# Two small changes at the ends of a fused attention and MLP kernel: the later packed queries load by a casting DMA on the GpSimd queue, and the last output tile is made as two column halves stored from two queues

## The chip, the cores and the metric

The kernel runs on one core of a Trainium2 chip. The metric is the device time of one execution in microseconds; lower is better. "The span" is the part of an execution that the profile covers, about 2 us shorter. "Same" means within 2%, so both the prediction and the result are about differences of about one per cent, and the traces carry the argument.

Engine names as the profile has them: PE is the tensor engine's matmuls, PEld its weight loads, DVE the vector engine, ACT the scalar engine, POOL the GpSimd engine, SP the engine that here only issues DMAs. POOLq, SPq and ACTq are the sequencers of those engines while they issue DMAs.

## The reference

For each of 8 batches and 8 heads, 32 packed queries `p` attend over 576 keys and values. The result serves as keys and values for the 576 queries `q`. Then a two-layer MLP with squared ReLU follows.

```python
def sm_attn(qq, kk, vv):                       # softmax attention, scale 1/8
    ...
p_packed = sm_attn(p, k, v)                    # p: 8 x 8 x 32 x 64
out = sm_attn(q, p_packed, p_packed)           # q, k, v: 8 x 8 x 576 x 64, float32
x = out.transpose(0, 2, 1, 3).reshape(4608, 512)
h = np.maximum(x @ w_in, 0.0)                  # w_in: 512 x 2048
return (h * h) @ w_out                         # w_out: 2048 x 512, output 4608 x 512 float32
```

## The kernel before

The program is written as streams of steps (load, transpose, scores, MLP matmuls and so on). When it is built, a small list scheduler (`Plan`) places the steps by assumed durations, and the order of their planned starts becomes the order of the instructions on each engine. Engines then run in order and wait on semaphores. So a step's assumed duration or its place in a stream can change the order of everything after it.

q, k, v, w_in and w_out are cast to bf16 by DMAs on the GpSimd queue, at most eight in flight, since each such load waits for the completion of the one eight before it. The packed queries are loaded in two parts, batches 0 and 1 first and batches 2 to 7 ("later p") afterwards. p is then transposed on DVE (`tr_p`) and expanded into a block-diagonal tile `pT_bd` on POOL (`expand_p`). The first score matmuls of a batch (`ps_a<-pT_bd,kT`) read that tile. Output tile t is 128 tokens x 512 columns, made of 16 matmuls (`f2_mm`).

```python
p_f = {}
def load_p(b0, b1, eng):                                     # float32, rows of 64 elements
    n = (b1 - b0) * NQD
    p_f[b0] = stg.tile([P, 2 * B, D], F32, name="p_f", tag="p")[:, :n, :]
    eng.dma_start(p_f[b0], p[b0:b1].rearrange("b (qd h) i d -> (h i) (b qd) d", h=QH))
def cast_p(b0, b1, eng):                                     # to bf16, on DVE
    ...
def tr_p(b0, b1):
    nc.vector.transpose(pT[:, b0 * NQD:b1 * NQD], p_b[b0].bitcast(F32))
def expand_p(b, eng):                                        # POOL for b > 0
    for h in range(QH):
        cast(eng, bd2(pT_bd[b % 2], h), pT[32 * h:32 * h + 32, ...]...)
# ... [cut]
def f2_out(t, eng):                                          # eng: ACT or DVE
    ob[t] = opool.tile([P, NE], F32, name="o_sb")
    cast(eng, ob[t], po[t])
    for i in range(4):
        b, j = divmod(t * 4 + i, JT)
        dst = out[b * S:(b + 1) * S, :].rearrange("(a j) e -> j a e", j=JT)[j]
        nc.sync.dma_start(dst, ob[t][32 * i:32 * i + 32, :])
# ... [cut]
def pload(b0, b1):
    if b0 == 0: ...                                          # ACT queue
    return Step(f"LP.{b0}", [stage([("SP", 0.45, lambda: load_p(b0, b1, nc.sync))]),
                             stage([("DMA", 1.6, lambda: None)])], [], [("p", 1)], (), lag=1.6)
ld = load_steps(0) + w_in_load() + w_out_load()[:2] + load_steps(1) + w_out_load()[2:]
for b in range(2, B):
    ld += load_steps(b) + ([pload(2, B)] if b == 2 else [])
```

The softmax here doesn't subtract the row's maximum and nothing guards it: scores larger than these inputs give would overflow.

Of the kernel before, what the change touches and what calls it, by code (L numbers as in the profile page):

```python
# [9 lines left out]
ACT = mybir.ActivationFunctionType  # L10
ALU = mybir.AluOpType
F32 = mybir.dt.float32
BF16 = mybir.dt.bfloat16

P = 128
D = 64
NP = 32
QH = 4
JT = 18
# [268 lines left out]
def kernel_impl(tc, q, k, v, p, w_in, w_out, out):  # L288
    nc = tc.nc
    B, H, S, Dh = q.shape  # L290
# [3 lines left out]
    NE = w_out.shape[1]  # L294
    NFB = DFF // FB
# [5 lines left out]
    NKQ = 8  # L301
    NT = TOK // P

    with ExitStack() as ctx:
        ctx.enter_context(tc.manual_schedule())
        consts = ctx.enter_context(tc.tile_pool(name="consts", bufs=1))
        stg = ctx.enter_context(tc.tile_pool(name="stg", bufs=1))
# [5 lines left out]
        opool = ctx.enter_context(tc.tile_pool(name="opool", bufs=3))  # L313
        ps_att = ctx.enter_context(tc.tile_pool(name="ps_att", bufs=2, space=bass.MemoryType.PSUM))
        ps_h = ctx.enter_context(tc.tile_pool(name="ps_h", bufs=2, space=bass.MemoryType.PSUM))
        ps_o = ctx.enter_context(tc.tile_pool(name="ps_o", bufs=2, space=bass.MemoryType.PSUM))
# [4 lines left out]
        w_out_b = consts.tile([P, NFB, NE], BF16, name="w_out_b")  # L321
# [24 lines left out]
        def cast(eng, dst, src):  # L346
            if eng is nc.scalar:
                nc.scalar.copy(dst, src)  # L348
            else:
                eng.tensor_copy(dst, src)  # L350
# [19 lines left out]
        def keep_clock(ps):  # L370
            for _ in range(plan.fill):
                nc.tensor.matmul(ps, lhsT=idle_b[:, :P], rhs=idle_b, start=True, stop=True)

        p_f = {}

        def load_p(b0, b1, eng):
            n = (b1 - b0) * NQD
            p_f[b0] = stg.tile([P, 2 * B, D], F32, name="p_f", tag="p")[:, :n, :]
            eng.dma_start(p_f[b0], p[b0:b1].rearrange("b (qd h) i d -> (h i) (b qd) d", h=QH))

        p_b = {}

        def cast_p(b0, b1, eng):
            n = (b1 - b0) * NQD
            p_b[b0] = stg.tile([P, 2 * B * D], BF16, name="p_b", tag="pb")[:, :n * D].rearrange("p (n d) -> p n d", d=D)
            cast(eng, p_b[b0], p_f[b0])

        def tr_p(b0, b1):
            nc.vector.transpose(pT[:, b0 * NQD:b1 * NQD], p_b[b0].bitcast(F32))
# [190 lines left out]
        gT = consts.tile([P, NFB, 2 * S], BF16, name="gT")  # L580
# [27 lines left out]
        po, ob = {}, {}  # L608
        WIDE2 = ()

        def f2_mm(t, fb):
            n0 = (t * P) % (2 * S)
            if fb == 0 and t in WIDE2:
                ps = ps_h.tile([P, 2, 512], F32, name="ps_w", tag="h")
                po[t], po[t + 1] = ps[:, 0], ps[:, 1]
            elif fb == 0 and t - 1 not in WIDE2:
                po[t] = ps_o.tile([P, NE], F32, name="ps_o", tag="o")
                keep_clock(po[t][:, :256])
            nc.tensor.matmul(po[t], lhsT=gT[:, fb, n0:n0 + P], rhs=w_out_b[:, fb, :],  # L619
                             start=(fb == 0), stop=(fb == NFB - 1))  # L620

        def f2_out(t, eng):
# [7 lines that stand above are left out]
        V, A, Q = nc.vector, nc.scalar, nc.gpsimd  # L630
# [3 lines left out]
        def cast_alt(n, engs, fn):  # L634
            return [(NAME[id(e)], COST[NAME[id(e)]][0] + n * COST[NAME[id(e)]][1] / 1000, lambda e=e: fn(e)) for e in engs]

        plan = Plan({"a": 2, "h": 2, "o": 2, "dl": 8, "p": 1, "pb": 1, "kqb": NKQ, "v": 2, "e2": 3, "r": 3,
                     "osb": 3, "ls": 2})


# [5 lines left out]
        def stage(*pieces):  # L646
            return list(pieces)

        def load_step(name, issue, us, fn, slot, deps=()):
            return Step(name, [stage([("POOL", issue, fn)]), stage([("-", 1.15, lambda: None)]), stage([("DMA", us, lambda: None)])],  # L650
                        deps, slot + [("dl", 1)], [("dl", 2, None)], lag=0.85)

        def load_steps(b):
            def kq(nm, qd):
                return load_step(f"L{nm}.{b}.{qd}", 0.56, 1.5, lambda: L[b].dma_kq(nm, qd), [("kqb", 1)])

            def vv(p, n):
                h0, h1 = p * H // n, (p + 1) * H // n
                return [load_step(f"Lv.{b}.{p}.{i}", 0.6, (0.82 if i < 2 else 0.66) / n,
                                  lambda i=i: L[b].dma_v(i, h0, h1), [("v", 1)] if p == 0 and i == 0 else [])  # L660
                        for i in range(4)]

            return [kq("k", 0), kq("k", 1)] + vv(0, 1) + [kq("q", 0), kq("q", 1)]

        def w_in_load():
            return [load_step(f"LWI.{fq}.{cp}", 0.72, 1.3, lambda fq=fq, cp=cp: dma_w_in(fq, cp), [])
                    for fq in range(NWC) for cp in range(2)]

        def w_out_load():
            return [load_step(f"LWO.{c}", 0.72, 1.3, lambda c=c: dma_w_out(c), []) for c in range(NFB // 2)]  # L670
# [92 lines left out]
        def f2_steps(t):  # L763
            bs = sorted({t * P // S, (t * P + P - 1) // S})
            res = [Step(f"F2.{t}.{fb}", [stage([("PE", 0.214, lambda fb=fb: f2_mm(t, fb))])],
                        [f"F1.{b}.{fb | 1}" for b in bs] + [f"LWO.{fb // 2}"], [("o", 1)] if fb == 0 else [])
                   for fb in range(NFB - 1)]
            fb = NFB - 1
            res.append(Step(f"F2.{t}.{fb}", [stage([("PE", 0.214, lambda: f2_mm(t, fb))]),
                                             stage([("ACT", 0.58, lambda: f2_out(t, A)), ("DVE", 0.64, lambda: f2_out(t, V))])],  # L770
                            [f"F1.{b}.{fb | 1}" for b in bs] + [f"LWO.{fb // 2}"], [("osb", 1)], [("o", 1, f"F2.{t}.0"), ("osb", 1, None)]))
            return res

        def f2_wide(t):
            bs = sorted({t * P // S, (t * P + 2 * P - 1) // S})
            res = []
            for fb in range(NFB):
                mm = stage([("PE", 0.43, lambda fb=fb: (f2_mm(t, fb), f2_mm(t + 1, fb)))])
                deps = [f"F1.{b}.{fb | 1}" for b in bs] + [f"F1.{b}.{NFB - 1}" for b in bs if fb == 0] + [f"LWO.{fb // 2}"]
                if fb < NFB - 1:  # L780
                    res.append(Step(f"F2.{t}.{fb}", [mm], deps, [("h", 1)] if fb == 0 else []))
                else:
                    res.append(Step(f"F2.{t}.{fb}", [mm, stage(*[[("ACT", 0.58, lambda u=u: f2_out(u, A)), ("DVE", 0.69, lambda u=u: f2_out(u, V))]
                                                                 for u in (t, t + 1)])],
                                    deps, [("osb", 2)], [("h", 1, f"F2.{t}.0"), ("osb", 1, None)]))
                res.append(Step(f"F2.{t + 1}.{fb}", [stage([("-", 0.0, lambda: None)])], [f"F2.{t}.{fb}"]))
            return res
# [6 lines left out]
        def pload(b0, b1):  # L794
            if b0 == 0:
                return Step("LP.0", [stage([("ACTQ", 0.5, lambda: load_p(b0, b1, A))])], (), [("p", 1)], (), lag=2.2)
            return Step(f"LP.{b0}", [stage([("SP", 0.45, lambda: load_p(b0, b1, nc.sync))]), stage([("DMA", 1.6, lambda: None)])],
                        [], [("p", 1)], (), lag=1.6)

        def pprep(b0, b1):  # L800
            n = (b1 - b0) * NQD * D
            return Step(f"P.{b0}", [stage(cast_alt(n, (V,), lambda e: cast_p(b0, b1, e))),
                                    stage([("DVE", 0.1 + n * 0.58 / 1000, lambda: tr_p(b0, b1))])],
                        [f"LP.{b0}"], [("pb", 1)], [("p", 0, f"LP.{b0}"), ("pb", 1, None)])

        NDV = 1
# [4 lines left out]
        setup()  # L811
        plan.base.update(DVE=2.5, POOL=0.8, ACT=0.5, SP=0.3, DMA=1.2, PE=3.6)
        plan.stream(0, [pload(0, 2)])
        ld = load_steps(0) + w_in_load() + w_out_load()[:2] + load_steps(1) + w_out_load()[2:]
        for b in range(2, B):
            ld += load_steps(b) + ([pload(2, B)] if b == 2 else [])
        plan.stream(0, ld)
        plan.stream(0.5, [Step("Z", [stage([("POOL", 2.6, setup_rest)])], ["Lq.0.1/1.0"])])
        plan.stream(1, [pprep(0, 2), pprep(2, B)])
# [9 lines left out]
        plan.stream(7, f2_steps(1))  # L829
        if WIDE2:  # L830
            plan.stream(7, f2_wide(2))
        plan.stream(7, sum([f2_steps(t) for t in range(4 if WIDE2 else 2, NT)], []))
        est = plan.run(ROUNDS, SEEDS)
@with_exitstack
def kernel(
# [41 lines left out]
```

## Time and profile before

| | before |
|---|---|
| time, median of 4 (range) | 259.03 us (258.76 to 259.27) |
| span of the profiled execution | 256.4 us |
| PE busy | 235.0 us, 92% of the span |
| first `ps_s` matmul (batch 0, second attention) | 18.11 us |
| first `ps_s` matmul of batch 1 | 40.57 us |
| end of the last matmul | 251.44 us |

PE is busy for 10.00 us in every ten-microsecond stretch from 50 to 250 us, and its matmul stream cannot be shortened by either part of the change. The busy time by ten-microsecond stretches of the kernel before shows it (columns: stretch, its length, then busy us and count of each engine, the granted clock, the DMA share and the GB/s that the DMA engines moved; the DMA share is the summed time of all packets over 16 engines, so it passes 1 where packets overlap):

```profile
0.00:10.00 10.00, 2.49 (x20) 1.97 (x20) 4.85 (x18) 2.75 (x4) 7.89 (x21) 1.00 0.92 139
10.00:20.00 10.00, 3.38 (x38) 2.40 (x38) 4.81 (x10) 1.65 (x5) 7.08 (x14) 1.00 1.20 201
30.00:40.00 10.00, 9.20 (x99) 6.37 (x97) 9.12 (x18) 7.59 (x17) 5.94 (x9) 1.00 1.24 203
40.00:50.00 10.00, 9.86 (x82) 4.93 (x82) 8.06 (x14) 7.60 (x13) 4.49 (x8) 1.00 1.24 204
50.00:60.00 10.00, 10.00 (x66) 6.21 (x64) 9.34 (x15) 6.92 (x12) 6.25 (x15) 1.00 1.20 230
```

Only the first 40 us have PE gaps, and there the DMA engines are busy throughout at about 204 GB/s (the first row is lower because nothing is in flight for its first 2 us). So three things can move the time: when the dense stretch begins, whether new gaps open in it, and the tail after its last matmul. I use one mark for the beginning: batch 1's first `ps_s` matmul, 40.57 us here. From it to the last matmul's end there are 251.44 - 40.57 = 210.87 us, and no wait is recorded within them.

Next, lines of the timeline of the kernel before (start, duration, engine, line, operation, operands; in brackets the engine's idle time before it and what ended it):

```profile
3.27 0.43 SPq L379 DMA_DIRECT2D p_f<-in_p_dram  x1
...
12.47 0.90 DVE L350 COPY v_b<-v_r 128x1280 bf16<-128x1280 bf16 x2 [4.49 <-DMA v_r<-in_v_dram]
...
18.11 2.12 PE L551 MATMUL ps_s<-qT,pq_bd 128*128 128x288 bf16 x8 [3.60 <-ACT pq_bd L348]
...
38.85 1.02 PE L619 MATMUL ps_o<-w_out_b,gT 128*128 128x512 bf16 x4 [0.35 <-DMA w_out_b<-in_moe_w_out_dram]
40.14 0.59 PE L619 MATMUL ps_o<-w_out_b,gT 128*128 128x512 bf16 x2 [0.27 <-DMA w_out_b<-in_moe_w_out_dram]
40.57 1.14 PE L551 MATMUL ps_s<-qT,pq_bd 128*128 128x288 bf16 x8
```

and the line of the DMA issues on its page (size, median us from issue to landing):

```profile
p_f<-in_p_dram SPq DMA_DIRECT2D x1, 384.0 KB, 14.5
```

The later p load, which the source lists after batch 2's loads, is issued at 3.27 us and takes 14.5 us. Nothing stands ahead of it on the SP queue, so only its staging tile (shared with the first p load) holds it. It is in flight while PE waits for v and then q of batch 0.

The tail, from the timeline of the kernel before:

```profile
251.53 0.59 ACT L348 COPY o_sb<-ps_o 128x512 f32<-128x512 f32 x1 [2.87 <-DMA out_dram<-o_sb]
252.14 1.72 SPq L628 DMA_DIRECT2D out_dram<-o_sb  x4
```

The copy starts 0.1 us after the last matmul. (The bracket names a store. The last copy starts 0.09 us after the last matmul's end, so I read it as waiting for the matmul.) The four store issues take 1.72 us in series, and the span ends at 256.4, which is 2.5 us after the last issue. From last matmul to span end: 256.4 - 251.44 = 4.96 us.

### The profile page before, as it was taken

The page shows a single profiled execution, that of the slowest core. Times are in us where ns is not written, and L with a number is a line of the kernel's source. Part 1 is how long each engine was busy: PE and PEld are TensorE (multiplying, and loading weights), DVE is VectorE, ACT ScalarE, POOL GpSimd, SP SyncE. Part 2 cuts the span into 40 slices and gives each one's busy share as a digit, 9 for nine tenths or more (in the row PEclk, how much of TensorE's full clock was granted, in tenths as well). Part 3 has the DMA queues.
Part 4 walks back from the last instruction along what each step waited for, and adds up shares of the span by engine and source line. Part 5 has one row for each costly group of instructions (what it writes and reads, how often), then busy time and mean ns, then how long its engine had stood idle before and what let it go on. Part 6 is the DMA issues. An engine that isn't in the chain of part 4 may idle for free.

```text
span 256.4 us, 4801 instructions
## 1 busy us (share of the span) xinstructions
PE 235.0 (92%) x1840; PEld 134.5 (52%) x1840; DVE 149.5 (58%) x263; ACT 157.6 (61%) x278; POOL 59.6 (23%) x120
## 2 busy tenths in 40 slices
PE   0348999999999999999999999999999999999992
PEld 0333574566655557646745764676346646544440
DVE  6166798797977679798857867684425205400000
ACT  2218778786678788877875877787727725611110
POOL 8855464549555002200700000000000000000000
PEclk9999999999999999999999999999999999999999
DMA  7999999999999913740972011102221121123222
GB/s 113 194 199 205 205 206 208 210 235 211 227 221 228 224 36 45 129 86 13 147 142 61 3 41 45 41 22 51 54 54 31 43 76 47 41 63 96 72 71 69
DMA packets 26678, 28.62 MB, mean 112 GB/s; under 512 B 5664, under 2 KB 17952, under 8 KB 26656
## 3 DMA queue, kind: packets, MB, share of 16 engines
q0 software_dynamic: 17664, 18.36, 43.8%
q1 hardware_dynamic: 8464, 9.84, 14.8%
q8 instruction: 14, 0.23, 0.4%
q10 hardware_dynamic: 528, 0.13, 0.2%
q14 instruction: 8, 0.07, 0.1%
HBM read 37.22 MB, written 9.44 MB: 182 GB/s over the span
## 4 chain that ended last, share of the span: by engine, by line
PE 76%; DMA 16%; SPq 2%; POOL 2%; ACT 1%; issue 1%; ACTq 0%; POOLq 0%
PE ps_o L619 42%; PE ps_h L589 22%; DMA k_b<-in_k_dram 6%; DMA w_in_b<-in_moe_w_in_dram 4%; PE ps_a L521 4%; DMA out_dram<-o_sb 3%; DMA w_out_b<-in_moe_w_out_dram 3%; PE ps_s L551 3%; SPq L628 2%; PE ps_a L455 2%; PE ps_pp L490 1%; PE ps_s L563 1%; ACT o_sb L348 1%; POOL w_in_b L418 1%; PE ps_a L469 1%
## 5 line engine op out<-in xcount | busy, mean ns | idle before, releaser
L619 PE MATMUL ps_o<-w_out_b,gT 128*128 128x512 bf16 x576 | 147.2, 379 | 0.6 <-DMA w_out_b<-in_moe_w_out_dram 0.6
L599 ACT ACTIVATE r<-ps_h 128x576 bf16<-128x576 f32 x126 | 79.9, 650 | 22.9 <-PE ps_h L589 17.8
L619 PEld LDWEIGHTS <-gT 128*128 128x128 bf16 x576 | 55.1, 98 | 52.2 <-issue 5.9
L589 PE MATMUL ps_h<-a,M 128*128 128x288 bf16 x512 | 80.0, 286 | 0.3 <-ACT r L599 0.3
L606 DVE TENSOR_TENSOR gT<-r 128x1152 bf16<-128x1152 bf16 x64 | 47.3, 751 | 29.7 <-PE ps_o L619 16.0
L589 PEld LDWEIGHTS <-M 128*128 128x128 bf16 x512 | 48.8, 98 | 25.8 <-issue 2.2
L531 DVE TENSOR_SCALAR M<-ps_a,rD 128x512 bf16<-128x512 f32 x38 | 27.9, 748 | 21.2 <-PE ps_a L521 21.2
L348 ACT COPY o_sb<-ps_o 128x512 f32<-128x512 f32 x20 | 11.7, 585 | 36.3 <-DMA out_dram<-o_sb 22.9
L410 POOL DMA_DIRECT2D v_r<-in_v_dram x32 | 18.8, 593 | 20.0 <-DVE gT L606 11.1
L529 ACT ACTIVATE M<-ps_a,rD 128x512 bf16<-128x512 f32 x26 | 17.6, 687 | 7.6 <-PE ps_a L521 7.6
L438 DVE STREAM_TRANSPOSE qT<-q_b 128x1152 bf16<-128x1152 bf16 x16 | 21.6, 1363 | 1.0 <-DMA q_b<-in_q_dram 0.8
L455 PE MATMUL ps_a<-pT_bd,kT 128*128 128x128 bf16 x128 | 9.8, 230 | 7.3 <-DVE kT L444 7.3
L521 PE MATMUL ps_a<-w_in_b,pp 64*32 64x512 bf16 x256 | 14.8, 400 | 1.1 <-DVE M L531 0.9
L444 DVE STREAM_TRANSPOSE kT<-k_b 128x320 f32<-128x320 f32 (+1 forms) x32 | 13.2, 454 | 4.0 <-DMA k_b<-in_k_dram 2.9
L348 ACT COPY pq_bd<-pp 32x64 bf16<-32x64 bf16 x32 | 7.7, 241 | 12.3 <-DVE pp L350 11.8
L405 POOL DMA_DIRECT2D q_b<-in_q_dram x16 | 8.9, 559 | 24.7 <-DVE qT L438 18.5
L558 ACT ACTIVATE e<-ps_s,rD 128x576 bf16<-128x576 f32 x16 | 11.2, 738 | 5.5 <-PE ps_s L551 5.5
L462 ACT ACTIVATE e<-ps_a 128x512 bf16<-128x512 f32 x16 | 9.0, 597 | 7.9 <-PE ps_a L455 7.8
L551 PE MATMUL ps_s<-qT,pq_bd 128*128 128x288 bf16 x64 | 10.5, 305 | 3.6 <-ACT pq_bd L348 3.6
L455 PEld LDWEIGHTS <-kT 128*128 128x128 bf16 x128 | 8.4, 103 | 9.3 <-DVE kT L444 8.3
L350 DVE COPY o_sb<-ps_o 128x512 f32<-128x512 f32 x16 | 11.0, 688 | 3.6 <-PE ps_o L619 3.5
L577 DVE TENSOR_TENSOR a<-e,ls 128x576 bf16<-128x576 bf16 x16 | 11.7, 754 | 1.0 <-ACT ls L571 1.0
(47 smaller groups left out, 140.4 us busy)
## 6 DMA issues: line engine op xcount, KB each, us to landing
out_dram<-o_sb SPq DMA_DIRECT2D x144, 64.0 KB, 1.7
k_b<-in_k_dram POOLq DMA_DIRECT2D x16, 288.0 KB, 9.1
q_b<-in_q_dram POOLq DMA_DIRECT2D x16, 288.0 KB, 8.5
v_r<-in_v_dram POOLq DMA_DIRECT2D x16, 160.0 KB, 9.4
v_r<-in_v_dram POOLq DMA_DIRECT2D x16, 128.0 KB, 8.7
w_in_b<-in_moe_w_in_dram POOLq DMA_DIRECT2D x8, 256.0 KB, 10.7
w_out_b<-in_moe_w_out_dram POOLq DMA_DIRECT2D x8, 256.0 KB, 9.0
p_f<-in_p_dram SPq DMA_DIRECT2D x1, 384.0 KB, 14.5
```

The costliest lines, as they stand in the source:

```text
L348: nc.scalar.copy(dst, src)
L410: nc.gpsimd.dma_start(self.vr[32 * i:32 * i + 32, h0:h1, :n * D], src[:, :, J0[i] * D:(J0[i] + n) * D])
L438: nc.vector.transpose(self.qT[:, qd].rearrange("p dh (j a) -> p j dh a", a=32), self.t.qb[qd][:].rearrange("p (j dh dl) -> p j dh dl", dh= ...
L455: nc.tensor.matmul(ps[:, g * P:(g + 1) * P], lhsT=self.kT[:, qd, g * P:(g + 1) * P].bitcast(BF16).rearrange("p (t two) -> p two t", two=2) ...
L521: nc.tensor.matmul(pss[qd][o:o + 32, :], lhsT=self.pp[64 * e:64 * e + 64, qd * P + pr * 64 + 32 * (e ^ qd):][:, :32], rhs=w_in_b[64 * e:64 ...
L529: nc.scalar.activation(dst, self.psm[c][e], ACT.Copy, scale=self.rD[:, e:e + 1])
L531: nc.vector.tensor_scalar_mul(dst, self.psm[c][e], self.rD[:, e:e + 1])
L551: nc.tensor.matmul(ps[:, c], lhsT=self.pq[:, blk(qd, dh)], rhs=self.qT[:, qd, dh, n0:n0 + HALF], start=(dh == 0), stop=(dh == 1))
L589: nc.tensor.matmul(ps[:, c, :HALF], lhsT=a.M[:, qd, fb * FB:(fb + 1) * FB], rhs=a.a2[:, qd, c * HALF:(c + 1) * HALF], start=(qd == 0), sto ...
L599: nc.scalar.activation(dst, src, ACT.Relu)
L606: eng.tensor_tensor(out=gT[:, fb - 1:fb + 1, o:o + S], in0=r, in1=r, op=ALU.mult)
L619: nc.tensor.matmul(po[t], lhsT=gT[:, fb, n0:n0 + P], rhs=w_out_b[:, fb, :], start=(fb == 0), stop=(fb == NFB - 1))
```

## The change

The intent has two parts. First, later p loads straight to bf16 by a casting DMA on the GpSimd queue, behind batch 2's k; the DVE cast goes away, and p's place among the other loads becomes real. Second, the last output tile is computed as two column halves, so that the first half's copy and stores run under the second half's matmuls, and the stores of each half go out from two queues.

```diff
@@ later p
-            p_f[b0] = stg.tile([P, 2 * B, D], F32, name="p_f", tag="p")[:, :n, :]
+            if eng is nc.gpsimd:
+                p_f[b0] = p_b[b0] = stg.tile([P, 2 * B * D], BF16, name="p_b", tag="pb")[...]
+            else:
+                p_f[b0] = stg.tile([P, 4, D], F32, name="p_f", tag="p")
@@ in pload and pprep
-            return Step(f"LP.{b0}", [stage([("SP", 0.45, lambda: load_p(b0, b1, nc.sync))]), ...
+            return load_step(f"LP.{b0}", 1.6, 1.6, lambda: load_p(b0, b1, Q), [("pb", 1)])
+            if b0:                                   # no DVE cast
+                return Step(f"P.{b0}", [stage(tr)], [f"LP.{b0}"], (), [("pb", 0, f"LP.{b0}")])
@@ order of the loads
-            ld += load_steps(b) + ([pload(2, B)] if b == 2 else [])
+            ld += load_steps(b)[:2] + ([pload(2, B)] if b == 2 else []) + load_steps(b)[2:]
@@ last tile
+        def f2_last(hf, fb):                         # 16 matmuls of 256 columns per half
+            ...
+        def f2_last_out(hf, eng):                    # half 0 on DVE, half 1 on ACT
+            cast(eng, o[:, :w], po[NT - 1, hf][:, :w])
+            for i in range(4):
+                ...
+                (nc.sync if i % 2 else nc.scalar).dma_start(dst, o[32 * i:32 * i + 32, :w])
-        plan.stream(7, sum([f2_steps(t) for t in range(4 if WIDE2 else 2, NT)], []))
+        plan.stream(7, sum([f2_steps(t) for t in range(4 if WIDE2 else 2, NT - 1)], []) + f2_last_steps())
```

The diff is cut: besides, the plan's number of `p_b` buffers goes from 1 to 2. The built programs show a third effect that the diff does not: the scheduler re-plans. PE's instruction order is the same up to about 46 us; then batch 2's first score matmuls come much earlier than before.

More of the change, by code (lines that the diff above doesn't have):

```diff
@@ L372, in keep_clock @@
                 nc.tensor.matmul(ps, lhsT=idle_b[:, :P], rhs=idle_b, start=True, stop=True)
-        p_f = {}
+        p_f, p_b = {}, {}
         def load_p(b0, b1, eng):
             n = (b1 - b0) * NQD
-            p_f[b0] = stg.tile([P, 2 * B, D], F32, name="p_f", tag="p")[:, :n, :]
+            if eng is nc.gpsimd:
+                p_f[b0] = p_b[b0] = stg.tile([P, 2 * B * D], BF16, name="p_b", tag="pb")[:, :n * D].rearrange("p (n d) -> p n d", d=D)
+            else:
+                p_f[b0] = stg.tile([P, 4, D], F32, name="p_f", tag="p")
             eng.dma_start(p_f[b0], p[b0:b1].rearrange("b (qd h) i d -> (h i) (b qd) d", h=QH))
-        p_b = {}
         def cast_p(b0, b1, eng):
@@ L609, in kernel_impl @@
         WIDE2 = ()
+        def f2_last(hf, fb):
+            n0 = ((NT - 1) * P) % (2 * S)
+            w = NE // 2
+            if fb == 0:
+                po[NT - 1, hf] = ps_o.tile([P, NE], F32, name="ps_o", tag="o")
+            nc.tensor.matmul(po[NT - 1, hf][:, :w], lhsT=gT[:, fb, n0:n0 + P], rhs=w_out_b[:, fb, hf * w:(hf + 1) * w],
+                             start=(fb == 0), stop=(fb == NFB - 1))
+        def f2_last_out(hf, eng):
+            w = NE // 2
+            o = opool.tile([P, NE], F32, name="o_sb")
+            cast(eng, o[:, :w], po[NT - 1, hf][:, :w])
+            for i in range(4):
+                b, j = divmod((NT - 1) * 4 + i, JT)
+                dst = out[b * S:(b + 1) * S, hf * w:(hf + 1) * w].rearrange("(a j) e -> j a e", j=JT)[j]
+                (nc.sync if i % 2 else nc.scalar).dma_start(dst, o[32 * i:32 * i + 32, :w])
         def f2_mm(t, fb):
@@ L635, in cast_alt @@
             return [(NAME[id(e)], COST[NAME[id(e)]][0] + n * COST[NAME[id(e)]][1] / 1000, lambda e=e: fn(e)) for e in engs]
-        plan = Plan({"a": 2, "h": 2, "o": 2, "dl": 8, "p": 1, "pb": 1, "kqb": NKQ, "v": 2, "e2": 3, "r": 3,
+        plan = Plan({"a": 2, "h": 2, "o": 2, "dl": 8, "p": 1, "pb": 2, "kqb": NKQ, "v": 2, "e2": 3, "r": 3,
                      "osb": 3, "ls": 2})
@@ L772, in f2_steps, with f2_last_steps @@
             return res
+        def f2_last_steps():
+            res = []
+            for hf in range(2):
+                for fb in range(NFB):
+                    st = [stage([("PE", 0.11, lambda fb=fb, hf=hf: f2_last(hf, fb))])]
+                    end = fb == NFB - 1
+                    if end:
+                        st.append(stage([("DVE", 0.35, lambda: f2_last_out(0, V)) if hf == 0 else ("ACT", 0.38, lambda: f2_last_out(1, A))]))
+                    res.append(Step(f"F2.{NT - 1}.{hf}.{fb}", st, [f"F1.{B - 1}.{fb | 1}"], [("o", 1)] if fb == 0 else [("osb", 1)] if end else [],
+                                    [("o", 1, f"F2.{NT - 1}.{hf}.0"), ("osb", 1, None)] if end else []))
+            return res
         def f2_wide(t):
@@ L796, in pload @@
                 return Step("LP.0", [stage([("ACTQ", 0.5, lambda: load_p(b0, b1, A))])], (), [("p", 1)], (), lag=2.2)
-            return Step(f"LP.{b0}", [stage([("SP", 0.45, lambda: load_p(b0, b1, nc.sync))]), stage([("DMA", 1.6, lambda: None)])],
-                        [], [("p", 1)], (), lag=1.6)
+            return load_step(f"LP.{b0}", 1.6, 1.6, lambda: load_p(b0, b1, Q), [("pb", 1)])
         def pprep(b0, b1):
             n = (b1 - b0) * NQD * D
-            return Step(f"P.{b0}", [stage(cast_alt(n, (V,), lambda e: cast_p(b0, b1, e))),
-                                    stage([("DVE", 0.1 + n * 0.58 / 1000, lambda: tr_p(b0, b1))])],
+            tr = [("DVE", 0.1 + n * 0.58 / 1000, lambda: tr_p(b0, b1))]
+            if b0:
+                return Step(f"P.{b0}", [stage(tr)], [f"LP.{b0}"], (), [("pb", 0, f"LP.{b0}")])
+            return Step(f"P.{b0}", [stage([("DVE", 0.29, lambda: cast_p(b0, b1, V))]), stage(tr)],
                         [f"LP.{b0}"], [("pb", 1)], [("p", 0, f"LP.{b0}"), ("pb", 1, None)])
```

## The prediction

> **What bounds the kernel now.** Busy time by ten-microsecond stretches shows the tensor engine 10.00 us busy in each from 50 to 250 us at a granted clock of 1.00; its last idle gap ends at 40.1 us. So only three things can move the time: how early that dense block starts, whether new gaps appear in it, and the tail. Before 40 us the chain of waits is DMA (k until 7.1, w_in until 21.2, k until 32.3, w_out until 40.1 us); the DMA engines are saturated from 2 to 90 us (about 204 GB/s). The tail, by the timeline: last matmul ends about 251.4, ACT copies the tile in 0.59 us, the SP queue issues four stores in 1.72 us (to 253.9), the last lands about 1.6 us later, span end 256.4.
>
> **What the change does.**
> 1. Later p load. The timeline shows the old 384 KB load issued at 3.27 us, not after batch 2 where the source lists it: the SP queue has nothing ahead of it. It lands 14.5 us later, amid the v, q and w_in loads that the tensor engine waits for. The Trainium skill ("DMA: Bandwidth & Descriptors", Issuing engines are not separate DMA queues) says all queues share 16 engines and interleave; this trace agrees: from 3.3 to 17.8 us they moved 191 GB/s (2.77 MB), 0.39 MB of it p, against 205 GB/s later. Estimate: the other loads lost (2.97-2.38) MB / 205 GB/s = 2.9 us at most, 1 us at least. Changed, p stands on the GpSimd queue behind batch 2's k, near 36 us. I expect the dense block 1.5 to 2.5 us earlier. The DVE cast (0.55 us at 54.4) goes; DVE is not the limit.
> 2. New risk. PE's order is unchanged up to about 46 us; then batch 2's first score matmuls come earlier, after 52.4 us of old-time work instead of 60.2, so near 50.4 us with the shift. They need p landed (issue about 37.4, 8 to 9 us in the queue, 1536 short packets: about 48.5), a transpose (0.58 us) and the POOL expansion (1.3 to 1.8 us, behind a v load): about 50 to 52 us. The DVE transpose also blocks the squares behind it; batch 2's q is tighter. I charge 0 to 2.5 us of new gaps between 46 and 60 us, 0.8 as a middle.
> 3. Last tile in halves. Sixteen 216 ns matmuls become 32 of half width; 288-column ones run 122 ns apart with weight loads hidden, so 256-column ones should take about 108: no cost. The first half's copy and stores hide under the second's matmuls. After the last matmul: ACT copy 0.38 (as a 128x256 activation) for 0.59, two issues per queue for four: saves 0.2+0.85 = about 1.0 us.
>
> **Sum.** 258.9 - 2.0 + 0.8 - 1.0 = about 256.7 us. Range 255.1 to 258.4. Faster by over 2%: 0.03; within 2%: 0.95; slower by over 2%: 0.02.
>
> **What would show each step.** p issued near 36 to 38 us on POOL; first v copy before 12.0 us (12.47 now), first ps_s matmul near 16.3 (18.11 now), dense from about 38 us; last matmul to span end about 4.0 us (5.0 now), half-width matmuls about 108 ns apart. For step 2: PE waiting for pT_bd from POOL, DVE pT for DMA p_b, or PE ps_s for ACT pq_bd at 48 to 60 us.
>
> **What would make it wrong.** If early landings are limited by issuing or compute rather than bandwidth, step 1 gives under 1 us. If the casting load of 256-byte rows takes much over 2 us of DMA or POOL time, the gap at batch 2 eats the gain. If the reordered middle has further gaps after 60 us, it gets slower.

## The result, and the profile after

| | before | after |
|---|---|---|
| time, median of 4 (range) | 259.03 us (258.76 to 259.27) | 256.16 us (255.71 to 257.02) |
| span of the profiled execution | 256.4 us | 255.2 us |
| first `ps_s` matmul | 18.11 us | 15.96 us |
| first `ps_s` matmul of batch 1 (mark) | 40.57 us | 38.41 us |
| mark to last matmul | 210.87 us | 213.01 us |
| last matmul to span end | 4.96 us | 3.78 us |

The ratio is 0.9893, with a 95% interval of 0.9863 to 0.9923. Ratios here are the mean time of one kernel's fast runs over that of the other's of the same rounds, so not quite the ratio of the medians quoted. The change is faster by 1.1%, inside the predicted range. The profiled execution of the changed kernel, at 257.02 us, was the slowest of its four. That of the kernel before took 258.20 us, less than any of its four timed runs above (it is a separate execution). So the two traces are only 1.2 us apart, while the medians are 2.87 us apart.

The table's last three rows add up to the span: 2.16 us gained at the start, 2.14 us lost in the dense stretch, 1.18 us gained in the tail. In this execution the start gain was given back completely.

The same stretches of the changed kernel; the stretches from 40 to 60 us now have gaps:

```profile
0.00:10.00 10.00, 2.50 (x20) 1.97 (x20) 4.71 (x18) 2.40 (x4) 7.52 (x21) 1.00 0.92 141
10.00:20.00 10.00, 5.30 (x51) 3.08 (x52) 6.29 (x12) 3.60 (x10) 8.61 (x17) 1.00 1.20 201
30.00:40.00 10.00, 9.64 (x103) 6.50 (x101) 9.01 (x18) 7.69 (x17) 6.62 (x10) 1.00 1.23 205
40.00:50.00 10.00, 9.22 (x71) 4.58 (x70) 7.85 (x14) 8.07 (x14) 3.27 (x7) 1.00 1.40 202
50.00:60.00 10.00, 9.09 (x103) 6.31 (x102) 8.30 (x16) 7.52 (x16) 7.40 (x19) 1.00 1.20 225
```

The lines of the changed kernel's timeline that answer to those shown of before:

```profile
10.71 1.09 DVE L350 COPY v_b<-v_r 128x1280 bf16<-128x1280 bf16 x2 [2.36 <-DMA v_r<-in_v_dram]
...
15.96 2.13 PE L552 MATMUL ps_s<-qT,pq_bd 128*128 128x288 bf16 x8 [3.21 <-ACT pq_bd L348]
...
37.98 0.59 PE L637 MATMUL ps_o<-w_out_b,gT 128*128 128x512 bf16 x2 [0.22 <-DMA w_out_b<-in_moe_w_out_dram]
38.41 1.14 PE L552 MATMUL ps_s<-qT,pq_bd 128*128 128x288 bf16 x8
...
44.11 1.24 PE L637 MATMUL ps_o<-w_out_b,gT 128*128 128x512 bf16 x5 [0.78 <-DMA w_out_b<-in_moe_w_out_dram]
...
52.44 1.05 PE L456 MATMUL ps_a<-pT_bd,kT 128*128 128x128 bf16 x16 [0.89 <-POOL pT_bd L350]
```

v's copy comes 1.8 us earlier, batch 0's `ps_s` 2.15 us and batch 1's 2.16 us earlier. Two new waits follow: for a piece of w_out (0.78 us) and for `pT_bd` (0.89 us). The bracketed idle time starts at the modelled end of the matmul before; the loss against back-to-back matmuls is about 0.17 us more per wait (a 512-column matmul is shown as 0.38 us, while in the dense stretch the next starts 0.216 us after it), so these two account for about 2.0 of the 2.14 us. The piece of w_out that the first one waits for is the last of the eight; it took 11.1 us from issue to landing here, against 9.8 us in the kernel before.

The later p load now, on the page of the changed kernel, and the chain of waits at batch 2 (start, duration, what):

```profile
p_b<-in_p_dram POOLq DMA_DIRECT2D x1, 192.0 KB, 12.1
```

```profile
36.99 12.09 DMA p_b<-in_p_dram
...
49.60 0.28 POOL k_b L406
...
50.43 0.60 POOL v_r L411
...
51.07 0.28 POOL pT_bd L350
...
52.10 0.30 POOL pT_bd L350
...
52.44 1.05 PE ps_a L456 x16
```

p lands at 49.07 us. Its expansion on POOL begins only at 51.07 us, after two load issues that stand ahead of it on that engine (49.60 and 50.43). The first of these two had itself waited for p, which held one of the eight places.

The tail of the changed kernel:

```profile
247.76 3.66 PE L617 MATMUL ps_o<-w_out_b,gT 128*128 128x256 bf16 x32
...
249.77 0.42 DVE L350 COPY o_sb<-ps_o 128x256 f32<-128x256 f32 x1 [26.91 <-PE ps_o L617]
250.22 0.83 ACTq L627 DMA_DIRECT2D out_dram<-o_sb  x2
250.44 2.23 SPq L627 DMA_DIRECT2D out_dram<-o_sb  x4
251.50 0.37 ACT L348 COPY o_sb<-ps_o 128x256 f32<-128x256 f32 x1 [2.91 <-DMA out_dram<-o_sb]
251.90 0.85 ACTq L627 DMA_DIRECT2D out_dram<-o_sb  x2
```

The half-width matmuls take (3.66 - 0.16)/32 = 0.109 us each, as estimated, and the first half's copy and the issues of its stores are done (251.28 us) before the last copy starts (251.50).

### The profile page after: what moved, and what is told of

Read it like the earlier page. It is cut to its first block, busy times and chain, and to the rows that moved or that the text cites. A ratio compares the mean times of both kernels' runs of the same rounds, so it can differ in the third digit from the quotient of the medians.

```text
span 255.2 us, 4833 instructions
## 1 busy us (share of the span) xinstructions
PE 235.5 (92%) x1856; PEld 136.5 (53%) x1856; DVE 147.1 (58%) x260; ACT 158.4 (62%) x281; POOL 58.9 (23%) x121
## 4 chain that ended last, share of the span: by engine, by line
PE 70%; DMA 19%; POOL 3%; SPq 3%; ACT 2%; issue 1%; DVE 1%; POOLq 0%
PE ps_o L637 38%; PE ps_h L590 20%; DMA p_b<-in_p_dram 5%; DMA k_b<-in_k_dram 4%; DMA out_dram<-o_sb 4%; DMA w_out_b<-in_moe_w_out_dram 3%; PE ps_a L522 3%; DMA q_b<-in_q_dram 3%; SPq L646 3%; PE ps_s L552 2%; PE ps_a L456 2%; ACT o_sb L348 2%; PE ps_pp L491 1%; PE ps_s L564 1%; POOL v_r L411 1%
## 5 line engine op out<-in xcount | busy, mean ns | idle before, releaser
L637 PE MATMUL ps_o<-w_out_b,gT 128*128 128x512 bf16 x560 | 143.1, 379 | 1.1 <-DMA w_out_b<-in_moe_w_out_dram 1.0
L637 PEld LDWEIGHTS <-gT 128*128 128x128 bf16 x560 | 53.1, 98 | 51.0 <-issue 6.9
L532 DVE TENSOR_SCALAR M<-ps_a,rD 128x512 bf16<-128x512 f32 x36 | 26.5, 748 | 17.8 <-PE ps_a L522 17.6
L348 ACT COPY o_sb<-ps_o 128x512 f32<-128x512 f32 (+1 forms) x22 | 12.6, 574 | 38.0 <-DMA out_dram<-o_sb 25.2
L350 DVE COPY o_sb<-ps_o 128x512 f32<-128x512 f32 (+1 forms) x15 | 10.0, 668 | 31.1 <-PE ps_o L617 26.9
L530 ACT ACTIVATE M<-ps_a,rD 128x512 bf16<-128x512 f32 x28 | 19.0, 688 | 7.4 <-PE ps_a L522 7.4
L456 PEld LDWEIGHTS <-kT 128*128 128x128 bf16 x128 | 8.5, 103 | 10.1 <-DVE kT L445 7.6
```

Source lines behind the costliest of these rows:

```text
L348: nc.scalar.copy(dst, src)
L456: nc.tensor.matmul(ps[:, g * P:(g + 1) * P], lhsT=self.kT[:, qd, g * P:(g + 1) * P].bitcast(BF16).rearrange("p (t two) -> p two t", two=2) ...
L530: nc.scalar.activation(dst, self.psm[c][e], ACT.Copy, scale=self.rD[:, e:e + 1])
L532: nc.vector.tensor_scalar_mul(dst, self.psm[c][e], self.rD[:, e:e + 1])
L637: nc.tensor.matmul(po[t], lhsT=gT[:, fb, n0:n0 + P], rhs=w_out_b[:, fb, :], start=(fb == 0), stop=(fb == NFB - 1))
```

## The experiments

There were twelve runs (e5 repeats the kernel of e2, e11 the changed kernel, e12 that of e4), e1 to e4 on one chip, e5 to e8 on another, e9 to e12 on a third, each beside runs of the kernel before. The kernel before had medians of 258.87, 258.88 and 258.71 us there. To hold the order of instructions fixed, I kept a step in the plan and changed only what it emits, or moved one emission; the instruction sequences of all engines were compared with those of the parent kernel before a run, and only the intended instruction differs. The traces bear this out for e1, e3, e6 to e10 and e12, leaving aside matmul records that some traces lack. The results of e6 and e8 are wrong on purpose. The results first:

| kernel | median us | ratio to before (95% interval) | first `ps_s` | mark | mark to last matmul | last matmul to end |
|---|---|---|---|---|---|---|
| e1 tail only | 257.82 | 0.9959 (0.9943, 0.9976) | 18.45 | 40.92 | 211.39 | 3.69 |
| e2 p only (five fast runs) | 257.66 | 0.9958 (0.9932, 0.9984) | no usable profile | | | |
| e3 p moved, old order | 256.47 | 0.9905 (0.9890, 0.9919) | 16.41 | 38.58 | 210.89 | 5.03 |
| e4 old order and tail | 255.35 | 0.9859 (0.9840, 0.9878) | 15.89 | 39.09 | 210.94 | 3.77 |
| e5 p only, again | 258.14 | 0.9972 (0.9954, 0.9990) | 16.23 | 40.33 | 211.85 | 5.02 |
| e6 no p DMA (wrong result) | 257.66 | 0.9956 (0.9943, 0.9969) | 16.00 | 39.32 | 211.74 | 5.04 |
| e7 expansion first | 257.38 | 0.9949 (0.9934, 0.9965) | 16.27 | 38.40 | 211.42 | 5.08 |
| e8 before without later p (wrong result) | 256.54 | 0.9928 (0.9895, 0.9961) | 16.33 | 41.01 | 210.88 | 5.11 |
| e9 casting load early | 259.25 | 1.0018 (0.9999, 1.0037) | 16.84 | 41.40 | 210.87 | 5.03 |
| e10 whole last tile, two queues | 258.29 | 0.9987 (0.9972, 1.0001) | 17.53 | 40.38 | 211.41 | 4.41 |
| e11 changed kernel again | 256.45 | 0.9917 (0.9901, 0.9933) | 16.34 | 38.66 | 212.17 | 3.77 |
| e12 old order and tail again | 255.19 | 0.9875 (0.9860, 0.9889) | 16.23 | 38.59 | 210.91 | 3.80 |

The last four columns are from the one profiled execution of each run.

### e1: the tail alone

```diff
 # kernel before, plus f2_last, f2_last_out, f2_last_steps of the change
-plan.stream(7, sum([f2_steps(t) for t in range(..., NT)], []))
+plan.stream(7, sum([f2_steps(t) for t in range(..., NT - 1)], []) + f2_last_steps())
```

> The kernel before with only the last tile in two halves; every other instruction is in the same order. If the two parts of the change are independent: start and dense block as before (first ps_s matmul near 18.1 us, last matmul near 251.4 us), last matmul to span end 3.8 us instead of 5.0, time 1.1 us less (about 257.9). If the tail gain is only seen because the start moved: under 0.4 us.

Measured: 1.05 us less by the medians, 3.69 us from last matmul to end. The tail's gain does not depend on the start.

### e2 and e5: the p part alone

```diff
 # changed kernel, last tile whole again
-plan.stream(7, sum([f2_steps(t) for t in range(..., NT - 1)], []) + f2_last_steps())
+plan.stream(7, sum([f2_steps(t) for t in range(..., NT)], []))
```

> The changed kernel with the last tile whole, as before. Independent parts: about 1.7 us less than before (257.3), made of about 2.3 us earlier dense block, less about 1.8 us of new waits of the tensor engine (w_out near 44, pT_bd near 52 us), less whatever the profiled run's clock drop at 22 to 26 us cost the profiled run alone. Rival, that p's move is worth nothing and the whole gain is the tail: within 0.5 us of before.

e2's profiled execution took 1354.96 us; its other five runs took 256.78 to 258.82 us. In it the large groups of matmuls are about three to four and a half times longer than in the other profiles, while DVE and ACT work as fast as elsewhere (the largest ACT group has a mean of 650 ns in e2 and in before). The record gives its granted clock as 1.00, but this trace holds no clock records at all, and its page has no PEclk row, so that number says nothing. By line and form, in e2:

```profile
L637 PE MATMUL ps_o<-w_out_b,gT 128*128 128x512 bf16 x576 | 806.2, 1695 | 0.0
```

The same group has a mean of 379 ns in the profiles of before and after. What happened there is not known, and nothing below rests on that execution.

> Run again because e2's profiled execution was a freak (1353 us). About 257.3 (1.7 us less than before); from e1 and e2's timed runs 1.1 to 1.7. In the trace: tensor engine waits for w_out near 44 us and for pT_bd near 52 us, together 1 to 2 us, that e3 (same loads, old order) does not have.

e5 measured 0.74 us less than before by the medians, e2's five fast runs 1.21; the ratios give 0.7 to 1.1 us. The expected 1.7 us was too much. The wait on `pT_bd` was there (0.70 us), the one on w_out near 44 us was not. So the p part keeps a third to a half of the 2.4 us that e3 shows the start could give.

### e3: the same load, the old order

```diff
 # kernel before; the plan's step for later p emits nothing on SP, the DVE cast emits nothing
+                if (self.b, name, qd) == (2, "k", 1):      # after batch 2's second k load
+                    load_p(2, B, nc.gpsimd)                # casting load, as in the change
```

> The kernel before, every engine's order kept, but the later p load issued as the casting GpSimd load behind batch 2's second k (and no DVE cast). Theory A (the new waits come from batch 2's score matmuls having been moved forward past p's landing): no wait on pT_bd, the dense block starts 2 us earlier and keeps it, 2.0 to 2.6 us less than before (about 256.7), better than e2. Rival B (the casting load of 256-byte rows costs about 2 us of saturated DMA time wherever it stands, and the later loads pass it on): waits of similar size appear in 42 to 60 us and it is equal to or slower than e2.

Measured: ratio 0.9905, 2.4 us less than before by the medians (2.0 us at the mark of the profiled execution), against 0.7 to 1.2 us for e2 and e5. Theory A fits. The mark stands at 38.58 us, the dense stretch is 210.89 us long as in the kernel before (210.87), and no wait on `pT_bd` appears. Rival B falls: the casting load ran here at the same place (issued 37.14, landed 10.2 us later) and nothing after it waited.

### e4: the old order with the tail

```diff
 # e3 plus the tail of e1
```

> e3 with the last tile in halves. Theory A and independent parts: 3.1 to 3.7 us less than before (about 255.6), half a microsecond faster than the changed kernel (256.2). Rival B: same as the changed kernel.

Measured: ratio 0.9859, 3.5 us less by the medians. The parts add: e3's 2.4 and e1's 1.05.

### e6: no later p DMA at all

```diff
 # e5; wrong result on purpose
+            if eng is nc.gpsimd:
+                nc.gpsimd.memset(p_b[b0], 0.0)
+                return
```

> Wrong result on purpose: the kernel of e5 with the later p load replaced by a fill of zeros on the same engine at the same place, so no p DMA at all. If p's arrival is what the new waits hang on: no wait on pT_bd near 52 us and no wait on w_out near 44 us, 1 to 2 us faster than e5, equal to or a little better than e3 (256.5). If the reordered plan is itself worse: the waits stay and it is no faster than e5.

This went against the first expectation. Without any p DMA, `pT_bd` is still waited for (0.60 us), the dense stretch is 211.74 us, 0.1 us shorter than e5's, and the time is 0.5 us less than e5's by the medians. p's landing is therefore not all that the wait hangs on. The timeline of e6 shows what else is there, POOL and DVE around 50 us:

```profile
49.65 2.42 POOL L350 COPY pT_bd<-pT 32x128 bf16<-32x128 bf16 x4 [0.82 <-DVE pT L393]
```

```profile
48.29 0.75 DVE L535 TENSOR_SCALAR M<-ps_a,rD 128x512 bf16<-128x512 f32 x1 [0.36 <-PE ps_a L525]
48.95 0.57 DVE L393 STREAM_TRANSPOSE pT<-p_b 128x384 f32<-128x384 f32 x1
49.45 1.48 DVE L610 TENSOR_TENSOR gT<-r 128x1152 bf16<-128x1152 bf16 x2
```

The transpose of p stands on DVE behind an `M` eviction that waits for PE (48.29), so it runs at 48.95 even with the data long there. In the changed kernel it ran at 49.10, 0.03 us after p's landing. And the four expansion copies take 2.42 us here instead of the 1.32 us of the changed kernel. What differs is what DVE does meanwhile: the first two copies overlap the two squares (`gT<-r`), which run from 49.45, and the last two overlap v's two copies (`v_b<-v_r`), which follow from 50.85; in the changed kernel nothing runs on DVE beside them. In the tile view of the changed kernel and of e6 (min/median/max ns of one copy):

```profile
L350 POOL COPY pT_bd<-pT x4: 280/286/292, 51.1 to 52.1; 32x128 bf16<-32x128 bf16 x4
```

```profile
L350 POOL COPY pT_bd<-pT x4: 438/548/709, 49.7 to 51.6; 32x128 bf16<-32x128 bf16 x4
```

The Trainium skill ("SBUF — State Buffer", SBUF: two separate sides) says that DVE and GpSimd share a port pair as an exclusive lock, which a DVE operation in a 2-port mode, or one with two SBUF inputs (this one against a GpSimd operation that reads SBUF, as the expansion does), can hold against GpSimd for a whole instruction. These traces agree: 286 ns a copy when DVE stands still, up to 709 ns beside squares of about 750 ns each. It is not that DVE is busy at all: in the changed kernel ten expansion copies between 51 and 60 us, six of them beside DVE transposes or `M` evictions, took 279 to 292 ns. That the lock is the cause is the page's account; no run separated it from other ways of slowing.

### e7: the expansion ahead of two load issues

```diff
 # e5; batch 3's second k load and first v load are emitted after batch 2's expansion
+            if b == 2:
+                for f in defer:
+                    f()
```

> The kernel of e5 with one thing moved: batch 2's expansion of p stands on the GpSimd queue ahead of the two load issues (batch 3's second k, first v) that it stood behind. In the changed kernel's trace p landed at 49.07, its transpose ended at 49.7, but the expansion began at 51.07 because those two issues waited (one of them for the queue slot that p itself held). Theory: the expansion starts near 49.8, the wait on pT_bd (0.9 us) goes, 0.7 to 1.0 us faster than e5. Rival: p's landing alone sets it; no gain.

Measured: 0.76 us less than e5 by the medians, but the ratio intervals (0.9934 to 0.9965 and 0.9954 to 0.9990) overlap a little, so this alone is not firm. The trace is clearer. The expansion begins at 48.71 us, directly after the transpose, and then runs beside the squares:

```profile
48.71 2.12 POOL L350 COPY pT_bd<-pT 32x128 bf16<-32x128 bf16 x4 [1.49 <-DVE pT L390]
```

It takes 2.12 instead of e5's 1.38 us, so of e5's 0.70 us of wait 0.30 us stay, and the dense stretch falls from 211.85 to 211.42 us. Taking away one obstacle mostly uncovers the next.

### e8: the kernel before without its early p load

```diff
 # kernel before; wrong result on purpose
+            if eng is nc.sync:
+                nc.gpsimd.memset(p_f[b0], 0.0)
+                return
```

> Wrong result on purpose: the kernel before with the early later-p load taken out (its staging tile is filled with zeros instead). If the early load's share of the DMA engines is the whole of e3's gain: first ps_s matmul near 16.2 us, dense from about 38 us, 2.2 to 2.8 us less than before, equal to e3 within 0.4 us. If e3 gains from something else (the DVE cast saved, the other queue): under 1 us.

Three of its four runs took 255.95 to 256.72 us; the profiled one took 258.75. The median is 2.3 us less than before, as e3's gain. The profiled execution has the early first `ps_s` (16.33 us), but then waits for w_in three times (0.51, 0.17 and 0.94 us) and reaches the mark late; at 2 us above the other three it is not typical of the timed runs. By the times, the early load is the whole of e3's gain, within the width of this interval. The traces show what it took: from 3 to 18 us the DMA engines moved 188 GB/s in the kernel before and 191 in e3, so about the same in all, but w_in's eight pieces took 10.7 us to land in the median before, 8.8 us in e3 and 8.2 us in e8.

### e9: the casting load early

```diff
 # e3 with
-                if (self.b, name, qd) == (2, "k", 1):
+                if (self.b, name, qd) == (0, "q", 1):
```

> e3 with the casting GpSimd load moved from behind batch 2's second k (37 us) to behind batch 0's q (about 5 us); nothing else differs. If it matters when p loads and not how: its DMA time falls before w_out again, the dense block starts 1.2 to 2 us later than in e3 (first ps_s early, near 16.3 us, because p stands behind q, but w_in and w_out late), about 258.0, under 1.3 us less than before. If the gain comes from the queue or from the half-sized write: as e3, 2.4 us less.

Slower than expected: 259.25 us, no gain at all over the kernel before and 2.8 us later at the mark than e3 (41.40 against 38.58). So the queue and the cast bring nothing as long as p loads early. PE's waits in e9 that e3 does not have:

```profile
21.70 0.41 PE L526 MATMUL ps_a<-w_in_b,pp 64*32 64x512 bf16 x7 [0.88 <-DMA w_in_b<-in_moe_w_in_dram]
22.99 0.39 PE L526 MATMUL ps_a<-w_in_b,pp 64*32 64x512 bf16 x1 [0.88 <-DMA w_in_b<-in_moe_w_in_dram]
24.27 0.62 PE L526 MATMUL ps_a<-w_in_b,pp 64*32 64x512 bf16 x7 [0.89 <-DMA w_in_b<-in_moe_w_in_dram]
```

The 2.8 us are not pure DMA time: from 18 to 24 us e9's DMA engines moved only 169 GB/s, against 205 in e3, and POOL issued w_in late: the second of its eight issues waits until 9.60 us for v to land (7.59 us in e3), and the last six begin at 13.32 us, after POOL's fills of constants (10.63 us in e3). How much of the 2.8 us is the load itself was not separated.

### e10: the last tile whole, from two queues

```diff
-                nc.sync.dma_start(dst, ob[t][32 * i:32 * i + 32, :])
+                (nc.scalar if t == NT - 1 and i % 2 == 0 else nc.sync).dma_start(dst, ...)
```

> The kernel before with the last tile whole, its four stores issued two from SP and two from ACT. Splits e1's 1.05 to 1.2 us: two issues fewer in series are worth 0.85 us, the half-length last copy 0.2 us. So 0.8 to 0.9 us less than before, last matmul to span end about 4.1 us (5.0 before, 3.7 in e1). Rival, that the two queues hold each other up: under 0.4 us.

Measured: 4.41 us from last matmul to end, 0.55 less than before, and 0.4 us less in time with an interval that reaches zero. That is less than the 0.85 us of issues saved. The two issues on ACT:

```profile
251.88 0.58 ACT L348 COPY o_sb<-ps_o 128x512 f32<-128x512 f32 x1 [2.87 <-DMA out_dram<-o_sb]
...
252.49 0.85 ACTq L628 DMA_DIRECT2D out_dram<-o_sb  x2
```

The last issue ends at 252.49 + 0.85 = 253.34 us and the span at 256.2, 2.9 us later instead of 2.5. The halves' further 0.6 us (3.78 against 4.41) is therefore more than the 0.2 us of the shorter copy: only half the bytes remain to be stored at the end. That reading is argued from the traces, not tested.

### e11 and e12: the changed kernel and the old order side by side

> The changed kernel beside e12 on one chip. About 2.5 us less than before (0.990), with runs spread over 1 us or more; a wait on pT_bd of 0.6 to 0.9 us near 52 us, and perhaps none on w_out near 44 us, which e5 did not have.

> e4 again beside the changed kernel: 3.4 us less than before (0.986 to 0.988), no wait on pT_bd, 0.8 to 1.4 us faster than the changed kernel of the same rounds. If e4's lead was that chip's luck: within 0.4 us of e11.

Measured on one chip: 256.45 us (ratio 0.9917) and 255.19 us (0.9875), intervals apart. The old order with both parts is 0.4% faster than the changed kernel; it beats the kernel before on two chips and the changed kernel where the two ran side by side. e11's dense stretch is 212.17 us, with waits of 0.51 us on w_out and 0.30 us on `pT_bd` (expected were 0.6 to 0.9 us on `pT_bd` and perhaps none on w_out); e12's is 210.91 us with neither. PE's waits after the mark, first e11, then the nearest two lines that e12 has:

```profile
38.23 0.59 PE L637 MATMUL ps_o<-w_out_b,gT 128*128 128x512 bf16 x2 [0.44 <-DMA w_out_b<-in_moe_w_out_dram]
...
44.10 1.24 PE L637 MATMUL ps_o<-w_out_b,gT 128*128 128x512 bf16 x5 [0.51 <-DMA w_out_b<-in_moe_w_out_dram]
...
51.85 1.05 PE L456 MATMUL ps_a<-pT_bd,kT 128*128 128x128 bf16 x16 [0.30 <-POOL pT_bd L350]
```

```profile
38.16 0.59 PE L641 MATMUL ps_o<-w_out_b,gT 128*128 128x512 bf16 x2 [0.47 <-DMA w_out_b<-in_moe_w_out_dram]
38.59 1.14 PE L556 MATMUL ps_s<-qT,pq_bd 128*128 128x288 bf16 x8
```

e12's only wait of this part lies before its mark. The wait for w_out near 44 us is settled in part: after and e11 have it, e5, e6 and e7 with the same order do not, and e1 and e10 with the old order have a smaller one near 46 us. In each of these four, PE goes on within 0.1 us of the landing of w_out's last piece. That piece took 11.1 us from issue to landing in after and 10.9 in e11, but 10.1 to 10.2 in e5, e6 and e7. It looks like scatter in a landing; what makes it late is not known.

## Why the prediction was right

1. **What bounds the kernel.** Right. The dense stretch is 210.87 to 210.94 us in before, e3, e4, e8, e9 and e12 (e1 and e10 lose 0.5 us more to one wait for w_out); start, gaps and tail account for the profiled spans.
2. **The later p load.** Right in mechanism and size. Predicted: dense stretch 1.5 to 2.5 us earlier, first `ps_s` near 16.3 us; measured: 2.16 us and 15.96 us. e3 (2.4 us) and e8 (2.3 us) show that taking p out of the first 18 us is worth that, and e9 that the cast and the queue bring no gain while the load stays early. By the traces the early load lengthened w_in's landings (10.7 us before, 8.8 in e3), as predicted from shared DMA engines.
3. **The new risk at batch 2.** Right in place and about right in the size of the wait that it named; one wait was missed, and the reason was half right. Predicted: 0 to 2.5 us between 46 and 60 us, 0.8 as a middle, for a chain of p's landing, transpose and expansion. Measured as loss of the dense stretch (each less 210.87): 2.14 us in the first trace, 1.30 us in e11 and 0.98 us in e5. The wait on `pT_bd`, with the 0.17 us above, is 1.06, 0.47 and 0.87 us of that. The wait for w_out near 44 us, which the prediction did not have, is 0.95 us in the first trace and 0.68 us in e11. p landed at 49.07 us, near the 48.5 predicted. But e6 shows that p's landing is not the only limit: with no DMA, 0.87 us are still lost. The scheduler moved batch 2's score matmuls to a place that the chain of eviction, transpose and expansion does not reach in time, whatever the load does. Three limits lie within about a microsecond: p's landing, the DVE order ahead of the transpose, and POOL, where load issues stand ahead of the expansion or squares slow it.
4. **The tail.** Right in sum (1.0 predicted, 1.18 in the trace, 1.05 in e1's time), wrong in its split: 0.85 us for the second queue and 0.2 us for the copy were predicted; e10 shows 0.55 us for the second queue, which leaves about 0.6 us for the halves.

The total of 256.7 us was 0.5 us above the first median and 0.25 us above e11's. That does not prove each term. In the first trace the terms sum to 2.16 - 2.14 + 1.18 = 1.20 us, a microsecond less than the 2.2 us predicted; in e11, profiled near its median, to 1.91 - 1.30 + 1.19 = 1.80 us. The medians differ by more than these sums (2.87 us, and 2.26 us beside e11), in part because the trace of the kernel before is of one of its fastest executions. So the mechanism is shown by the experiments, but that the total came so close is partly luck.

Two further points. The stretch from first `ps_s` to the mark, which holds nearly the same instructions in all kernels with p behind batch 2's k, took 22.1 to 24.1 us in their profiles. A clock drop at 22 to 26 us (0.57 in the changed kernel) does not explain it, since e12 without a drop and the changed kernel with one took 22.4 us each. POOL's waits go with it. In before, after, e1, e3, e7, e11 and e12 (22.1 to 22.5 us) POOL waits about 0.7 us before each of the two q issues of batch 1. In e4, e5, e6 and e8 (23.2 to 24.7 us) one of these waits is 2.1 to 2.4 us, for an early piece of w_out that holds one of the eight places and took 10.8 to 12.5 us to land (9.2 to 10.3 us in the first group). e10 lies between (1.4 us, 22.9 us); e9 has the cause told above. First the changed kernel, then e5, where both q issues follow the late piece:

```profile
25.56 0.56 POOL L406 DMA_DIRECT2D q_b<-in_q_dram  x1 [0.67 <-DMA w_out_b<-in_moe_w_out_dram]
```

```profile
28.29 1.20 POOL L406 DMA_DIRECT2D q_b<-in_q_dram  x2 [2.39 <-DMA w_out_b<-in_moe_w_out_dram]
```

e4 has it and e12, the same kernel, has not, so it scatters from execution to execution; why a piece lands late is not known. The profiled executions of e5 and e8 are the slowest of their runs, which fits, and their marks in the table should be read with this in mind. What stays open is why e2 and e5 are slower in time than e3 by more than the 0.96 us that the dense stretches of e5 and e3 differ by: the timed runs have no traces, so it is not known how often a late landing hit them.

## What to carry to other kernels

A load on an otherwise empty queue starts as soon as its buffer is free, whatever its place in the source; look in the trace for when it was really issued, and ask what it takes from the loads that the critical engine is waiting for. Where a scheduler orders instructions from assumed times, a local change re-orders the rest; run the change once with the old order to know which part gained, as here the old order kept 1.1 to 1.3 us that the new one lost. When several limits end within a microsecond of each other, removing the one that the profile names gives little, so take away its whole cause, here the early place of the matmuls.

## What the Trainium skill lacked or had wrong

- "DMA: Bandwidth & Descriptors", Issuing engines are not separate DMA queues: the page states that queues share the engines and that several queues save only issue time; this section gives no size for either. The runs agree and add a size: p's 0.39 MB on another queue delayed batch 1's `ps_s` by 2.0 us (e3 against before), and of 0.85 us of issue time saved by a second queue 0.55 us remained (e10), because the span ended 2.9 instead of 2.5 us after the last issue.
- "SBUF — State Buffer", SBUF: two separate sides: agrees in direction; it gives no figure for small GpSimd copies beside bf16 `tensor_tensor` squares. Here 286 ns became up to 709 ns (expansion for batch 2 in e6).
- "TensorE: Matmul & The Clock Gate" has no case like e2: matmuls over four times longer (1695 instead of 379 ns in the largest group) through a whole execution of 1355 us, in a trace without clock records. What caused it is not known (one execution).
